# Delta-rule attention and an expert layer in one kernel: the first group's scores from stacked keys, half-block products in 64x64 tiles, other work order in the first steps

## The chip, the cores and the metric

The kernel runs on one core of one Trainium2 chip. The metric is the device time of one execution in microseconds. The time before is the median of three runs, 635.75 us (631.23 to 637.58). All data is 32-bit floating point; in the trace every matmul of the source stands as two matmul records and two weight loads.

## The reference, cut to what matters

Two parts follow one another. The first is a linear attention with the delta rule: for each of 4 batches and 8 heads a 48x48 state is walked over 768 tokens. Its output, 3072 rows of 384, is the input of the second part, in which each row goes to one of 8 experts (chosen by the largest gate logit) through two matrices with a ReLU between them.

```python
# attention: B, H, S, D = 4, 8, 768, 48
k_n = k / (norm(k) + 1e-06)
for t in range(S):
    y[t] = q[t] @ state
    v_old = state.T @ k_n[t]
    state = state + beta[t] * outer(k_n[t], v[t] - v_old)
# x = y as (3072, 384); experts: E = 8, F = 1024
expert = argmax(x @ w_gate); gate = softmax(x @ w_gate)[expert]
out = gate * (relu(x @ w1[expert]) @ w2[expert])
```

## The kernel before

The tokens are cut into 24 chunks of 32 (`C`), the chunks into groups of 4 (`GS`). A chunk is one **step**; the four batches lie on the 128 partitions, 32 tokens each. Per chunk and head a 32x32 triangular matrix, built from the products of the keys with each other, has to be inverted. VectorE does this for a group of 4 chunks at a time (`invert`), for all batches, tokens and heads side by side, in some seventy small operations, while the steps of the group ahead run. `fill` puts a number of microseconds of this work, by an estimate of its own, between the parts of a step.

The scores of a chunk are products of its keys with its keys (`k = 0`) and queries (`k = 1`), made by TensorE in 32x32 blocks. Two heads are stacked on 96 partitions; to keep them apart, the right-hand side is a "wide" copy with zeros where the other head's rows are. In the main loop those wide copies come from DRAM by DMA, half of each, into buffers that were zeroed once. For the first group, keys and queries are loaded as 48 partitions, one head each, and are not stacked:

```python
    def load_plain(c, k):
        t = kq_buffer()[0:D].rearrange("d p k t -> d (p k) t")
        for e, eng in enumerate((nc.sync, nc.scalar)):
            eng.dma_start(out=t[:, NP * e : NP * e + NP, :], in_=kq_t[c, D * e : D * e + D, :, k, :])
        return t
    ...
    def load_wide(c):
        if c < NS:
            for e in range(2):
                r = slice(D * e, D * e + D)
                nc.sync.dma_start(out=wide_kq[c % 3][r, e], in_=kq_t[c, r])
    ...
    def plain_scores(pa, keys, others):            # L348
        for h in range(H):
            for b in range(B):
                j = NP * (h % 2) + h // 2
                nc.tensor.matmul(
                    pa[rows_of(b), C * h : C * h + C], lhsT=keys[:, j, rows_of(b)],
                    rhs=others[:, j, rows_of(b)], start=True, stop=True, skip_group_check=True,
                )
    def front_scores(c, pa):                       # L359
        wide = wide_kq[c % 3]
        for p in range(NP):
            for b in range(B):
                for e in range(2):
                    nc.tensor.matmul(
                        pa[rows_of(b), 128 * p + 64 * e : 128 * p + 64 * e + 64],
                        lhsT=wide[:, e, p, 0, rows_of(b)], rhs=wide[:, e, p, :, rows_of(b)],
                        start=True, stop=True, skip_group_check=True,
                    )
        load_wide(c + 3)
        return c, pa
```

`scores` (L375) does the same for a later chunk with the stacked keys on the left. `keep_scores` (L399) and `keep_plain` (L388) mask the scores into `km` on VectorE.

The first group is inverted as two half blocks of 16. What lies between the halves is put together by `across`, with two small products per chunk on TensorE (L527), an eviction on ScalarE, and an addition on VectorE (L541). It runs as **chores**, one call at a time: for chunk 0 ahead of step 0, for chunks 1 to 3 within steps 0 to 2.

```python
        def product(l, r):
            po = psA.tile([128, 512], FP32, name="pa", tag="pa")
            for h in range(H):
                for b in range(B):
                    nc.tensor.matmul(
                        po[rows_of(b), W * h : W * h + W], lhsT=l[rows_of(b), H * s + h],
                        rhs=r[rows_of(b), h], start=True, stop=True, skip_group_check=True,
                    )
            return po[:, 0 : H * W]
```

`spread_out` (L558) then makes the block-diagonal copies `ubw` of the inverse on ScalarE, two operations for a whole group (for a chunk in the first group), each with a scale per partition of 0 or 1. A step begins with the values (`pv`, L595), takes off what the state holds (L609), evicts it as `R` (L620), multiplies by the inverse (`pz`, L631), evicts `Z` (L638), updates the state's sum (`acc`, L659) and the state (L667), and ends with the output (`pq`, L678), the scores of a later chunk and the start of the next step. The beginning of the kernel is this (shortened):

```python
    keys = [load_plain(c, 0) for c in range(GS)]
    ...                                            # constants, zeroing of the wide buffers
    for c in range(GS, GS + 3):
        load_wide(c)
    queries = [load_plain(c, 1) for c in range(GS)]
    ...
    for c in range(GS):
        ...
        plain_scores(pa, keys[c], keys[c])
        keep_plain(c, 0, pa[:, 0 : H * C], mask_0)
    behind.append([0, invert(0), 0.0])
    ahead = [front_scores(GS, acc[:, 2, :]), front_scores(GS + 1, acc[:, 3, :])]
    ...
    for c in range(GS):
        a = H * C * (c % 2)
        plain_scores(acc[:, c // 2, a : a + H * C], keys[c], queries[c])
    ...                                            # front_scores of GS + 2, GS + 3
    heat(3)                                        # L584: products of the identity, their result unused
    while not spread:
        fill(0.1)                                  # the inversion of group 0
    scale_v(0, 0); scale_v(0, 1)
    begin(0)
    chore()                                        # first half-block product
    ...
    chore(); ...; chore()                          # second product, addition
    spread_out((0, 1))
    ...
    for c in range(NS):
        ...
        extra = step(c)
        fill(4.0)
        ...
        more = score()
        if c + 1 < NS:
            begin(c + 1)
        fill(3.2)
        keep_scores(*more)
        if c == GS:                                # weights of expert 0, a piece per step
            weights[0] = start_w(wpool)
            pieces.extend(pieces_w(moe_w1[0], moe_w2[0], *weights[0]))
```

After the last step come the experts, one after another, on TensorE.

Of the kernel before, what the change touches and what calls it, by code (L numbers as in the profile page):

```python
# [31 lines left out]
E = 8  # L32
# [21 lines left out]
def _f32_consts():  # L54

    p = np.arange(128)[:, None]
    j = np.arange(128)[None, :]
    rev = np.broadcast_to(E - np.arange(E), (128, E))
    base = np.broadcast_to(np.arange(E) * LIST, (128, E))
    more = np.arange(E)[:, None] * LIST + CAP + np.arange(MAXR)[None, :] * 128
    more = np.broadcast_to(more.reshape(1, -1), (128, E * MAXR))
    t, w = p % C, j[:, :C]
    kk = 1.0 * (t == w) - (t < w)
    own = 1.0 * (p // C % 2 == np.arange(2)[None, :])
    half = t // (C // 2) == w // (C // 2)  # L70
    k0 = 1.0 * (t == w) - ((t < w) & half) - (t // (C // 2) > w // (C // 2))
    kq = -1.0 * (t < w)
    mine = -1.0 * (p // D == np.arange(2)[None, :])
    return np.concatenate(
        [kk, kq, k0, own, mine, rev, base, more, p < j, np.ones((128, 128))], axis=1
    ).astype(np.float32)
# [3 lines left out]
def kernel(  # L80
# [23 lines left out]
    CS = 3 * C + 4  # L104
# [3 lines left out]
    def part(w):  # L108
# [4 lines left out]
    mask, mask_0, own, mine, rev, base, further, upper, ones = (  # L113
        part(w) for w in (2 * C, C, 2, 2, E, E, E * MAXR, 128, 128)
# [164 lines left out]
    scored, front, now = [0], [None], [0]  # L279
# [34 lines left out]
    def load_plain(c, k):  # L314

        t = kq_buffer()[0:D].rearrange("d p k t -> d (p k) t")
        for e, eng in enumerate((nc.sync, nc.scalar)):
            eng.dma_start(out=t[:, NP * e : NP * e + NP, :], in_=kq_t[c, D * e : D * e + D, :, k, :])
        return t
# [6 lines left out]

    def load_wide(c):
        if c < NS:
            for e in range(2):
                r = slice(D * e, D * e + D)  # L330
                nc.sync.dma_start(out=wide_kq[c % 3][r, e], in_=kq_t[c, r])
# [11 lines left out]
    def plain_scores(pa, keys, others):  # L343

        for h in range(H):
            for b in range(B):
                j = NP * (h % 2) + h // 2
                nc.tensor.matmul(  # L348
                    pa[rows_of(b), C * h : C * h + C], lhsT=keys[:, j, rows_of(b)],
                    rhs=others[:, j, rows_of(b)], start=True, stop=True, skip_group_check=True,  # L350
                )

    def front_scores(c, pa):

        wide = wide_kq[c % 3]
        for p in range(NP):
            for b in range(B):
                for e in range(2):
                    nc.tensor.matmul(  # L359
                        pa[rows_of(b), 128 * p + 64 * e : 128 * p + 64 * e + 64],  # L360
                        lhsT=wide[:, e, p, 0, rows_of(b)], rhs=wide[:, e, p, :, rows_of(b)],
                        start=True, stop=True, skip_group_check=True,
                    )
        load_wide(c + 3)
        return c, pa

    def scores(c):

        if c >= NS:
            return None  # L370
        wide, kq = wide_kq[c % 3], kqs[c]
        pa = psA.tile([128, 512], FP32, name="pa", tag="pa")
        for p in range(NP):
            for b in range(B):
                nc.tensor.matmul(  # L375
                    pa[rows_of(b), 128 * p : 128 * p + 128], lhsT=kq[:, p, 0, rows_of(b)],
                    rhs=wide[:, :, p, :, rows_of(b)], start=True, stop=True,
                    skip_group_check=True,
                )
        load_wide(c + 3)  # L380
        return pa
# [135 lines left out]
    def across(gt, fdt, ub, s):  # L517

        W = C // 2
        part = ub[:, H * s : H * s + H, W:C]  # L520
        m1 = work.tile([128, H, W], FP32, name="m1")

        def product(l, r):
            po = psA.tile([128, 512], FP32, name="pa", tag="pa")
            for h in range(H):
                for b in range(B):
                    nc.tensor.matmul(  # L527
                        po[rows_of(b), W * h : W * h + W], lhsT=l[rows_of(b), H * s + h],
                        rhs=r[rows_of(b), h], start=True, stop=True, skip_group_check=True,
                    )  # L530
            return po[:, 0 : H * W]

        po = product(gt, part)
        nc.scalar.activation(out=m1[:].rearrange("p h w -> p (h w)"), in_=po, func=AF.Copy)

        def second():
            po = product(fdt, m1)
            chores.appendleft(partial(added, po))

        def added(po):  # L540
            nc.vector.tensor_tensor(  # L541
                out=part, in0=part, in1=po.rearrange("p (h w) -> p h w", h=H), op=OP.add
            )

        chores.appendleft(second)
# [5 lines left out]
    def spread_out(steps=(0, GS)):  # L551

        g, ub = spread[0]
        if g not in ubs:
            ubs[g] = block.tile([128, GS * H, 2, C], FP32, name="ubw")
        a, b = (H * s for s in steps)
        for k in range(2):
            nc.scalar.activation(  # L558
                out=ubs[g][:, a:b, k], in_=ub[:, a:b], func=AF.Copy, scale=own[:, k : k + 1]
            )  # L560
        if steps[1] == GS:
            spread.popleft()
# [38 lines left out]
    def step(c):  # L601
        g, s = divmod(c, GS)
        kq, ub, kt, vs, km = kqs.pop(c, None), ubs[g], kts.pop(c), vss.pop(c), kms[g]
# [38 lines left out]
        if c > 0:  # L642
            by_state(pq, 1, True)
        if c >= LATE:
            ranked()
            while turned:
                logits()
        if c == NS - 1:
            ahead_of_time(1)
        load_kq(c + LEAD + 1)  # L650
        if c < GS:
            load_kq(c + GS)
        extra = score() if c in EXTRA else None
        scale_v(c + 1, 1)
        if c < NS - 1:
# [10 lines left out]
            for e in range(2):  # L666
                nc.scalar.activation(  # L667
                    out=states[:, :, :, e], func=AF.Copy, scale=mine[0:DD, e : e + 1],
                    in_=acc[0:DD, :, 0:DM].rearrange(
                        "q b (p e w) -> q b p e w", p=NP, e=2  # L670
                    )[:, :, :, e],
                )
# [11 lines left out]
        if c == ss[0]:  # L684
            n = len(ss)
            xgs[c] = work.tile([128, n, ROW], FP32, name=f"xg{n}", bufs=3 if n == 1 else 2)
            lgs[c] = small.tile([128, GS, E], FP32, name="lg")
# [3 lines left out]
        if spread and GS <= c and c >= GS * (spread[0][0] - 1):  # L691
            spread_out()
        return extra

    def score():
        c = scored[0]
        scored[0] += 1
        return c, scores(c)
# [133 lines left out]
    keys = [load_plain(c, 0) for c in range(GS)]  # L832
    nc.scalar.dma_start(out=cf[:, 0:CS], in_=src[:, 0:CS])
    nc.scalar.dma_start(out=beta[:], in_=beta_blk)
    for i in (1, 2, 0):
        t = wide_kq[i][:].rearrange("q e p k w -> q (e p k w)")
        for j, eng in enumerate(((nc.vector, nc.gpsimd), (nc.gpsimd, nc.vector))[i % 2]):
            eng.memset(t[:, 1024 * j : 1024 * j + 1024], 0.0)
    for c in range(GS, GS + 3):
        load_wide(c)  # L840
    queries = [load_plain(c, 1) for c in range(GS)]
# [3 lines left out]
    load_vt(0)  # L845
    load_kt(0)
    for c in range(1, LEAD + 1):
        kqs[c] = kq_buffer()
    load_kq(1)

    kms[0] = km_buffer()
    for c in range(GS):
        pool, name = ((psA, "pa"), (psQ, "pq"), (psC, "pv"), (psC, "pz"))[c]
        pa = pool.tile([128, 512], FP32, name=name, tag=name)
        plain_scores(pa, keys[c], keys[c])
        keep_plain(c, 0, pa[:, 0 : H * C], mask_0)
    behind.append([0, invert(0), 0.0])
    ahead = [front_scores(GS, acc[:, 2, :]), front_scores(GS + 1, acc[:, 3, :])]
    load_vt(1)
    load_kt(1)  # L860
    for c in range(GS):
        a = H * C * (c % 2)
        plain_scores(acc[:, c // 2, a : a + H * C], keys[c], queries[c])
    load_kq(2)
    ahead.append(front_scores(GS + 2, psC.tile([128, 512], FP32, name="pv", tag="pv")))
    load_kq(8)
    ahead.append(front_scores(GS + 3, psQ.tile([128, 512], FP32, name="pq", tag="pq")))
    load_kq(9)
    load_kq(3)
    heat(3)  # L870
# [5 lines left out]
    chore()  # L876
    keep_plain(0, 1, acc[:, 0, :], mask[:, C : 2 * C])
# [4 lines left out]
    spread_out((0, 1))  # L882
# [12 lines left out]
    for c in range(NS):  # L895
# [3 lines left out]
        if c % GS == 0 and c // GS not in ubs:  # L899
            while not spread:  # L900
                fill(0.1)
            spread_out()
        extra = step(c)
        fill(4.0)
        if extra:
            keep_scores(*extra)
        if c < GS - 1:
            chore()
            spread_out((c + 1, c + 2))
# [9 lines left out]
        fill(3.2)  # L919
        keep_scores(*more)  # L920
        if c == GS:
# [193 lines left out]
```

## Time and profile before

| what | value |
|---|---|
| median of three runs | 635.75 us |
| span of the profiled execution | 630.8 us |
| step 0's first product (`pz`) starts | 43.71 us |
| `pz` of step 4 starts | 100.00 us |
| `Z` of the last step | 296.16 us |
| PE busy from 330 to 610 us | 279.73 of 280 us |
| VectorE busy from 0 to 297 us | 200.97 us |
| ScalarE busy from 0 to 44 us | 4.40 us |

The span has three parts. Up to 43.71 us is a prologue: loads, the scores of two groups, the inversion of the first. Then come 24 steps to about 297 us. Then, after an overlap of some 20 us, the experts, in which TensorE has no gap. A row of the profile names the line of the kernel, the engine, the operation, the tiles out and in, and the shape; "idle before" with a releaser says how long the engine stood before it and what ended the wait. The releaser "issue" means that nothing shown in the profile was waited for.

### The profile page before, as it was taken

Reading aid. Unit: us, or ns where it says so; the run is one execution under the profiler, and the core shown is the slowest. Engines: PE = TensorE matmul, PEld = TensorE weight load, DVE = VectorE, ACT = ScalarE, POOL = GpSimd, SP = SyncE. Lnnn points to the kernel's source line nnn. Section 1 sums busy time; section 2 is a strip of 40 time slices with the busy share of each in tenths; the row PEclk is TensorE's granted clock in tenths of the full one; section 3 lists DMA queues with packets and bytes.
Section 4 is the critical chain, followed back from the end, with each engine's and each line's share of the span. In section 5 each row is a group of like instructions: output and inputs, shape, how many; then the busy total and the mean of one; then the engine's idle time right before and its main releaser. Section 6 shows DMA issues by size and latency. Waiting matters only on the chain. (4 is left out here: it accounts for less than half of the span.)

```text
span 630.8 us, 17552 instructions
## 1 busy us (share of the span) xinstructions
PE 560.4 (89%) x7660; PEld 371.1 (59%) x7661; DVE 249.0 (39%) x818; ACT 184.2 (29%) x474; POOL 105.1 (17%) x111
## 2 busy tenths in 40 slices
PE   4378888879889899788999999999999999999990
PEld 4356666767767677566867555555555555455550
DVE  4845567997999979311410201111011110201100
ACT  0214536565465665563201101011011110111100
POOL 3000000010110202121137004014140231401011
PEclk9997758897888987685799999999999999999996
DMA  9857535676584322221017634223343223400000
GB/s 167 171 129 211 130 106 133 187 157 176 155 156 116 92 80 64 40 66 40 14 28 278 223 111 146 86 74 131 124 151 103 83 94 125 150 8 32 1 23 14
DMA packets 41632, 68.97 MB, mean 109 GB/s; under 512 B 10758, under 2 KB 31670, under 8 KB 41552
## 3 DMA queue, kind: packets, MB, share of 16 engines
q1 hardware_dynamic: 34128, 57.05, 33.4%
q0 software_dynamic: 4640, 9.47, 4.7%
q10 hardware_dynamic: 2784, 1.29, 1.2%
q8 instruction: 61, 1.00, 0.7%
q14 instruction: 19, 0.16, 0.1%
HBM read 59.02 MB, written 10.35 MB: 110 GB/s over the span
## 5 line engine op out<-in xcount | busy, mean ns | idle before, releaser
L993 PE MATMUL phe<-xTe,w1t 128*128 128x448 f32 (+1 forms) x384 | 136.2, 515 | 0.0
L1009 PE MATMUL pye<-w2t,hT 128*128 128x384 f32 x352 | 114.8, 486 | 0.0
L993 PEld LDWEIGHTS phe<-xTe,w1t 128*128 128x128 f32 x384 | 71.0, 190 | 60.4 <-issue 58.5
L1009 PEld LDWEIGHTS pye<-w2t,hT 128*128 128x128 f32 x352 | 66.9, 190 | 47.1 <-issue 2.6
L809 POOL DMA_INDIRECT lists<-ids,ri x24 | 24.0, 1001 | 277.8 <-DVE tmp L492 142.5
L998 DVE TENSOR_SCALAR hT<-phe 128x448 f32<-128x448 f32 (+1 forms) x32 | 18.9, 592 | 116.4 <-PE phe L993 104.3
L497 DVE TENSOR_TENSOR ut<-ut,tmp 128x58 f32<-128x58 f32 (+9 forms) x164 | 53.1, 324 | 5.4
L492 DVE TENSOR_TENSOR tmp<-ut 128x58 f32<-128x58 f32 (+9 forms) x164 | 52.8, 322 | 5.2
L180 POOL DMA_INDIRECT out_dram<-y,rows x22 | 21.9, 997 | 183.4 <-ACT y L1018 154.1
L571 ACT ACTIVATE vs<-vt,normt 128x48 f32<-128x48 f32 x192 | 47.9, 325 | 1.8 <-issue 1.8
L1002 ACT ACTIVATE hT<-phe 128x448 f32<-128x448 f32 (+1 forms) x32 | 16.6, 517 | 105.7 <-PE phe L993 105.7
L667 ACT ACTIVATE states<-acc,cf 96x768 f32<-96x768 f32 x46 | 38.7, 891 | 21.8 <-PE acc L659 19.4
L1018 ACT ACTIVATE y<-pye,xin 128x384 f32<-128x384 f32 x15 | 8.7, 581 | 122.5 <-PE pye L1009 122.5
L631 PE MATMUL pz<-R,ubw 64*64 64x48 f32 x736 | 29.9, 237 | 14.5 <-ACT lg L733 8.0
L988 DVE COPY xTe<-px 128x448 f32<-128x448 f32 (+1 forms) x24 | 13.3, 580 | 66.5 <-PE px L984 55.9
L631 PEld LDWEIGHTS pz<-R,ubw 64*64 64x64 f32 x736 | 26.8, 151 | 18.0 <-ACT lg L733 9.2
L678 PE MATMUL pq<-Z,km 32*32 32x48 f32 x1536 | 31.7, 230 | 6.3 <-issue 6.1
L678 PEld LDWEIGHTS pq<-Z,km 32*32 32x32 f32 x1536 | 25.5, 125 | 13.0 <-issue 12.6
L659 PE MATMUL acc<-Z,kt 32*96 32x96 f32 x736 | 29.1, 311 | 2.8 <-issue 1.5
L1014 DVE TENSOR_SCALAR y<-pye,xin 128x384 f32<-128x384 f32 x7 | 4.3, 618 | 68.3 <-PE pye L1009 68.3
L609 PEld LDWEIGHTS pv<-states,kq 96*32 96x32 f32 x736 | 17.4, 121 | 18.8 <-issue 11.7
L659 PEld LDWEIGHTS acc<-Z,kt 32*96 32x96 f32 x736 | 24.4, 210 | 6.4 <-issue 3.6
(142 smaller groups left out, 641.3 us busy)
## 6 DMA issues: line engine op xcount, KB each, us to landing
w1t<-in_moe_w_dram SPq DMA_DIRECT2D x7, 1536.0 KB, 12.3
w2t<-in_moe_w_dram SPq DMA_DIRECT2D x7, 1536.0 KB
kq<-in_kq_t_dram SPq DMA_DIRECT2D x23, 384.0 KB, 6.2
wkq<-in_kq_t_dram SPq DMA_DIRECT2D x40, 192.0 KB, 4.0
vt<-in_v_tok_dram SPq DMA_DIRECT2D x24, 192.0 KB, 2.9
kt<-in_k_tok_dram SPq DMA_DIRECT2D x24, 192.0 KB, 4.3
xs<-xg SPq DMA_DIRECT2D x24, 192.0 KB, 7.1
w1t<-in_moe_w_dram SPq DMA_DIRECT2D x6, 256.0 KB
```

What stands on the lines that cost most here:

```text
L180: nc.gpsimd.indirect_dma_start(out=out, out_offset=bass.IndirectOffsetOnAxis(ap=index, axis=0), in_=y[0:w, :], in_offset=None, bounds_chec ...
L492: nc.vector.tensor_tensor(out=tv, in0=ud[:, :, j + 1 : W, j].unsqueeze(3).to_broadcast([128, K, n, j]), in1=ud[:, :, j, 0:j].unsqueeze(2). ...
L497: nc.vector.tensor_tensor(out=ud[:, :, j + 1 : W, 0:j], in0=ud[:, :, j + 1 : W, 0:j], in1=tv, op=OP.add)
L571: nc.scalar.activation(out=vss[c][:, h, :], in_=vts[c][:, h, :], func=AF.Copy, scale=norms[g][:, H * s + h : H * s + h + 1],)
L631: nc.tensor.matmul(pz[r, D * h : D * h + D], lhsT=ub[r, H * s + h].rearrange("q k w -> q (k w)"), rhs=R[r, h, :], start=(h == 0), stop=Tru ...
L659: nc.tensor.matmul(acc[0:DD, b, DD * p : DD * p + DD], lhsT=kt[rows_of(b), 2 * p : 2 * p + 2, :], rhs=Z[rows_of(b), 2 * p : 2 * p + 2, :], ...
L667: nc.scalar.activation(out=states[:, :, :, e], func=AF.Copy, scale=mine[0:DD, e : e + 1], in_=acc[0:DD, :, 0:DM].rearrange("q b (p e w) -> ...
L678: nc.tensor.matmul(pq[rows_of(b), D * h : D * h + D], lhsT=km[rows_of(b), H * s + h, 1], rhs=Z[rows_of(b), h, :], start=(c == 0 and h == 0 ...
L809: nc.gpsimd.indirect_dma_start(out=lists, out_offset=bass.IndirectOffsetOnAxis(ap=ri[:, i : i + 1], axis=0), in_=ids[:, ss[i] : ss[i] + 1] ...
L993: nc.tensor.matmul(ph[:], lhsT=w1t[:, s, f * 128 : f * 128 + 128], rhs=xT[:, s, :], start=(s == 0), stop=(s == NK - 1),)
L998: nc.vector.tensor_scalar(out=hT[:, f, :], in0=ph[:], scalar1=0.0, scalar2=None, op0=OP.max)
L1009: nc.tensor.matmul(py[:], lhsT=hT[:, f, t * 128 : t * 128 + w], rhs=w2t[:, f, :], start=(f == 0), stop=(f == NF - 1),)
```

## The change

It does these things, all in the attention part:

- Keys and queries of the first group are loaded stacked on 96 partitions (`load_half`), into the buffers that the steps use later, so the second loading of chunks 1 to 3 goes. The wide copies for chunks 0 to 7 are made from them on chip: two operations with a scale of 0 or 1 per partition, on ScalarE, a few on VectorE. Zeroing the wide buffers and loading them from DRAM for chunks 4 to 7 go.
- All scores of the prologue then use the stacked form, with half as many matmuls.
- The half-block products take block-diagonal copies of the left side, made by `both` on ScalarE for chunk 0 and on GpSimd for chunks 1 to 3, and work in 64x64 tiles, with half as many matmuls.
- ScalarE's function table is loaded at the start by an operation on a dummy tile.
- Idle products (`heat`), to keep TensorE at work, are put in at waits: a fourth one in the prologue, three around the first half-block products and step 0, and one in each step that has no scores left to make.
- Up to step 9 `fill` takes 4.6 and 4.0 us of inversion per step in place of 4.0 and 3.2. The block-diagonal copies of the inverse are made chunk by chunk in every group. The first expert's weights are loaded from step 9 on instead of step 4.

```diff
+    def load_half(c, k, eng):
+        if c not in kqs:
+            kqs[c] = kq_buffer()
+        eng.dma_start(out=kqs[c][:, :, k, :], in_=kq_t[c, :, :, k, :])
...
+    def widen(c):
+        for e in range(2):
+            nc.scalar.activation(
+                out=wide_of(c)[:, e], in_=kqs[c][:], func=AF.Copy, scale=this[0:DD, e : e + 1]
+            )
...
+    def widen_half(c, k, w, i):
+        for e in range(2):
+            out, in_ = w[:, e, :, i, :], kqs[c][:, :, k, :]
+            if e or k:
+                nc.scalar.activation(out=out, in_=in_, func=AF.Copy, scale=this[0:DD, e : e + 1])
+            else:
+                nc.vector.tensor_scalar(
+                    out=out, in0=in_, scalar1=this[0:DD, 0:1], scalar2=None, op0=OP.mult
+                )
...
+    def half_scores(c, pa, w, i):
         for p in range(NP):
             for b in range(B):
+                nc.tensor.matmul(
+                    pa[rows_of(b), 64 * p : 64 * p + 64], lhsT=kqs[c][:, p, 0, rows_of(b)],
+                    rhs=w[:, :, p, i, rows_of(b)], start=True, stop=True, skip_group_check=True,
+                )
...
+        l1, l2 = (both(t[:, H * s : H * s + H], pool=s > 0) for t in (gt, fdt))
         def product(l, r):
             po = psA.tile([128, 512], FP32, name="pa", tag="pa")
             for h in range(H):
-                for b in range(B):
+                for q in two_of:
                     nc.tensor.matmul(
-                        po[rows_of(b), W * h : W * h + W], lhsT=l[rows_of(b), H * s + h],
-                        rhs=r[rows_of(b), h], start=True, stop=True, skip_group_check=True,
+                        po[q, W * h : W * h + W], lhsT=l[q, h].rearrange("q k w -> q (k w)"),
+                        rhs=r[q, h], start=True, stop=True, skip_group_check=True,
                     )
...
+    def both(of, out=None, pool=False):
+        if out is None:
+            out = work.tile([128, H, 2, C], FP32, name="bw", tag="bw", bufs=3)[:]
+        for k in range(2):
+            if pool:
+                nc.gpsimd.tensor_scalar(
+                    out=out[:, :, k], in0=of, scalar1=own[:, k : k + 1], scalar2=None, op0=OP.mult
+                )
+            else:
+                nc.scalar.activation(
+                    out=out[:, :, k], in_=of, func=AF.Copy, scale=own[:, k : k + 1]
+                )
+        return out
...
         if c > 0:
             by_state(pq, 1, True)
+        else:
+            heat(1, pq[:])
...
-        if spread and GS <= c and c >= GS * (spread[0][0] - 1):
-            spread_out()
+        if c >= GS - 1:
+            spread_out(c + 1)
...
     def score():
         c = scored[0]
         scored[0] += 1
+        if c >= NS:
+            heat()
         return c, scores(c)
...
     kms[0] = km_buffer()
+    w = (wide_kq[0], wide_kq[1])
     for c in range(GS):
+        if c % 2 == 0:
+            for i in range(2):
+                widen_half(c + i, 0, w[c // 2], i)
         ...
-        plain_scores(pa, keys[c], keys[c])
+        half_scores(c, pa, w[c // 2], c % 2)
         keep_plain(c, 0, pa[:, 0 : H * C], mask_0)
     behind.append([0, invert(0), 0.0])
...
-    heat(3)
+    heat(4)
     while not spread:
         fill(0.1)
     ...
     begin(0)
     chore()
+    heat(1, front[0][1][:])
     ...
     chore()
+    heat(1, front[0][1][:])
-    spread_out((0, 1))
+    spread_out(0)
...
-        fill(4.0)
+        fill(4.0 if c > LEAD else 4.6)
...
-        fill(3.2)
+        fill(3.2 if c > LEAD else 4.0)
...
-        if c == GS:
+        if c == LEAD:
```

## The prediction

> **What bounds the kernel now.** I read the page first, then the timeline of the first 60 us, then the table of windows cut at the steps, then the waits of VectorE.
>
> ```profile
> span 630.8 us, 17552 instructions
> PE 560.4 (89%) x7660; PEld 371.1 (59%) x7661; DVE 249.0 (39%) x818; ACT 184.2 (29%) x474; POOL 105.1 (17%) x111
> ...
> PEclk9997758897888987685799999999999999999996
> DMA  9857535676584322221017634223343223400000
> ...
> q8 instruction: 61, 1.00, 0.7%
> ```
>
> One slice is 15.8 us. TensorE ("PE") is near full from slice 19 on: that is the expert part, from about 320 us to 620 us, with the clock at 9 or more. The change touches no instruction there. So whatever it is worth lies before 300 us, in the attention part, and there PE's share is a poor guide: the clock digit drops to 5 and the DMA digit is 5 to 9 for the first twelve slices. The q8 line says that instructions themselves come by DMA: 1.00 MB in 61 packets is 16.4 KB a packet, and 7660 + 7661 PE instructions over 61 packets is 251 a packet, some 126 pairs of weight load and matmul.
>
> ```profile
> 11.80 0.68 PE L348 MATMUL pz<-kq 48*32 48x32 f32 x33 [2.11 <-issue]
> ...
> 12.41 3.13 PE L359 MATMUL acc<-wkq 96*32 96x64 f32 x93
> ...
> 18.30 1.38 PE L359 MATMUL acc<-wkq 96*32 96x64 f32 x35 [2.76 <-issue]
> ...
> 24.77 1.93 PE L348 MATMUL acc<-kq 48*32 48x32 f32 x128 [3.66 <-issue]
> ...
> 30.00 1.02 DVE L509 STREAM_TRANSPOSE fdt<-ut 128x512 f32<-128x512 f32 x1
> 30.97 0.74 PE L348 MATMUL acc<-kq 48*32 48x32 f32 x35 [4.26 <-issue]
> ...
> 36.08 4.39 PE L584 MATMUL pa<-ident 128*128 128x512 f32 x6
> ...
> 40.53 0.73 PE L527 MATMUL pa<-ub,km 32*32 32x16 f32 x64
> ...
> 42.42 0.29 DVE L541 TENSOR_TENSOR ub<-ub,pa 128x128 f32<-128x128 f32 x1 [8.79 <-PE pa L527]
> ...
> 43.71 1.14 PE L631 MATMUL pz<-vs,ubw 64*64 64x48 f32 x32 [1.34 <-ACT ubw L558]
> ```
>
> This is the prologue. VectorE ends the inversion of the first group at 31.02 us (30.00 + 1.02). The product that needs it (L527) starts at 40.53: 9.5 us later, although nothing it reads is missing. PE is in order and still works off scores and three heating products. Those are late because PE stops for 2.1 to 4.3 us with the releaser "issue", in the middle of runs of like matmuls, after exactly 128 pairs (93 + 35, then 128): a packet of instructions each. From 11.80 to 30.97 a packet takes 6.1 to 6.5 us while its 128 pairs need 2 to 4.5 us of work. So in the prologue **the instruction fetch of PE, behind a DMA that is 83 to 95% busy, sets the path**, and the 768 pairs of scores ahead of the heating (8 blocks of 64, 4 of them for queries, and 4 of 64 for the second group) are what is fetched.
>
> ```profile
> 44.00:57.37 13.37, 10.52 (x321) 8.03 (x317) 10.04 (x37) 5.96 (x17) 0.00 (x0) 0.62 0.80 217
> 57.37:71.81 14.44, 11.92 (x363) 9.17 (x364) 8.55 (x25) 6.46 (x19) 0.00 (x0) 0.76 0.45 118
> 71.81:87.80 15.99, 12.19 (x363) 9.29 (x363) 9.45 (x27) 6.45 (x19) 0.00 (x0) 0.76 0.49 136
> 87.80:100.00 12.20, 10.12 (x235) 8.21 (x235) 7.50 (x21) 7.35 (x18) 0.00 (x0) 0.75 0.42 116
> 100.00:109.30 9.30, 9.04 (x235) 7.34 (x235) 6.56 (x28) 5.39 (x16) 0.00 (x0) 0.82 0.48 126
> ```
>
> Columns: window, length, then PE, PEld, DVE, ACT, POOL busy with counts, clock, DMA share, GB/s. Steps 0 to 3 take 13.4, 14.4, 16.0 and 12.2 us; a later one takes 9 to 11. The long ones carry 128 extra pairs for the half-block products. The VectorE waits tell the rest:
>
> ```profile
> DVE ub L541 <- PE pa L527: 19.7, 4, 8.8
> ```
>
> 8.8 us of these 19.7 are the prologue's; the other 10.9 stand in steps 0 to 2 (1.5, 5.0, 4.4), where VectorE, in order, waits for the half-block product that PE does at a step's end, instead of inverting group 1. As a result group 1's inversion ends in step 3, and PE waits 2.1 us before step 4 for its copies.
>
> **What the Trainium skill says.** "Runtime: NRT & Kernel Launch", section "Instruction fetch mechanics": instructions are refilled in blocks of 16 KiB, 256 instructions, by a DMA of the sequencer's own, and the cost is mostly hidden. The trace agrees with the block (251 per packet) and not with "hidden" (the four gaps above are 12.8 us). "TensorE: Matmul & The Clock Gate", the part on the HAM clock gate: without sustained work the clock falls to half. Here the same pv<-vs product takes 0.91 us warm and 1.65 us cold, and the clock column is 0.62 to 0.76 in steps 0 to 3. "ScalarE: Activation LUTs", section "What ACT_TABLE_LOAD costs": about 1.28 us for a load; the trace has 1.28 us at 20.64, off the path, so moving it forward is worth nothing by itself.
>
> **The change part by part.**
>
> 1. Scores of group 0 and 1. Keys of two heads stacked on 96 rows instead of 48 halve the pairs: 4 x 64 becomes 4 x 32 for keys, the same for queries, and the second group's 4 x 64 becomes 4 x 32 of 128 columns. 768 pairs become 384, that is three packets less, 3 x 6.2 us of fetching. The DMA shrinks too: wide loads of 393 KB for chunks 4 to 7 go (1.57 MB) and so do the whole loads of chunks 1 to 3 (1.18 MB). At the 160 to 210 GB/s of the first windows 2.75 MB is about 14 us of DMA time, spread over 0 to 60 us.
>
> 2. ScalarE pays for it. A 128x1024 copy is 1.13 us (ubw, the row L558), a 128x256 one 0.49, so 0.83 ns an element and about 0.71 us for 512. Eight copies of 1024 are 9.0 us, four key copies of 512 are 2.8 us, eight for queries 5.7 us. ScalarE did nothing before 20.6 us, so this lies in idle time, but in a chain: keys land near 9 us, their last copy near 10, the copies of chunks 4 to 7 end near 19, of the queries near 25, the last scores near 26.
>
> 3. The start of the inversion. Before, it began at 12.98, because the last key block stood at 11.80 behind the first fetch. With 32 pairs a block, all key scores fit ahead of the point (223 pairs) where that fetch was needed. But each key has a copy of 0.7 us before it. I take 11.5 us, with the unchanged 18.0 us of VectorE: end near 29.5.
>
> 4. Heating and the first half-block product. Four products, by the measured 4.39 us for three, are 5.9 us: 26 to 32 us. So heating, not the inversion, is likely the last thing ahead of the product, by 2 us. Then product 0.6, its eviction 0.3, a heating product 1.2 to 1.5, second product 0.6, addition 0.3, copies 0.9: pz of step 0 near 35.3 instead of 43.7. **Gain 8.5 us**.
>
> 5. Steps 0 to 2. The half-block products in 64x64 tiles take 64 pairs a step instead of 128: half a packet, and a packet costs about 5.2 us here (14.44 us for 363 pairs, or 2.8 packets). That is 2.6 us a step, 7.8 in all, less about 1 us for the idle product put into step 0. The DMA carries 0.39 MB a step less. The mask copies go to POOL, which is empty here. VectorE now gets 4.6 + 4.0 us of inversion a step instead of 4.0 + 3.2; by the order of its instructions its half-block addition comes three pairs of operations later in step 1 and three in step 2, so of the 10.9 us of waiting I expect 3 to 4 to stay. Its own work, some 9.5 us a step, then bounds a step at about 11.5 us: (13.4 + 14.4 + 16.0) - 3 x 11.5 = **9.3 us**.
>
> 6. Step 3 and the copies for step 4. The last four transposes of group 1 stand before the masking of step 3 instead of around it, and the 2.19 us of copies are cut into 0.9 us per step. The 2.1 us before step 4 goes, giving 12.2 -> 10.7: **1.5 us**.
>
> 7. Steps 4 to 14. VectorE is 85 to 91% busy in 120 to 240 us, so these stay near 10 us. The first expert's weights move from steps 4 to 17 to steps 9 to 22, which frees DMA early and loads it late where its share was only 0.25 to 0.33: **0 to 2 us**.
>
> 8. Steps 15 to 23. A 512-column product is put in where the scores have run out, near 1.2 us warm. While VectorE bounds (to about 250 us) it is free; in the last four steps PE bounds and pays about 1 us each. Against that stand the 0.69 clock of 256 to 297 us: at half speed when cold, that is some 60% of the stretch cold. I set the sum at **0**, between +5 and -6.
>
> Sum: 8.5 + 9.3 + 1.5 + 1 + 0 = 20.3 us. 635.75 - 20.3 = 615.5; I say 616.
>
> **Rivals.** (a) ScalarE or the stacked keys' landing becomes the prologue's bound. For: the copies are a serial 17.5 us, and the 512-byte rows of the keys share the engines with rows of 4 KB. Against: 12 us of slack between 31.0 and 43.7. It would leave 4 of the 8.5 us, the total near 621. (b) Steps 0 to 3 are bound by VectorE alone and its waits only move to other products; then the halved pairs bring nothing and the total is near 624. For: VectorE still waits in order. Against: its busy time there is 7.5 to 10 us of 12 to 16. (c) The idle products cost their full 9 x 1.2 us late and never lift the clock: total near 625. (d) The clock does rise, and the cold half of 256 to 297 us shrinks: near 608.
>
> **Range and chances.** The prologue may miss by 3, steps 0 to 3 by 5, the late steps by 6, and the time before itself spans 631.23 to 637.58. Together about 9 us: 605 to 628. Faster by over 2% means under 623.0, which holds unless two rivals act together: 0.77. Within 2%: 0.21. Slower: 0.02.
>
> **What would show it.** pz<-vs,ubw of step 0 starts at 34 to 37 us; "issue" gaps on PE before it fall from four long ones to one or two; the addition of half blocks waits under 6 us in total; windows of steps 0 to 3 take 10.5 to 12.5 us; the step-4 wait for copies is gone; the clock in 256 to 297 us is at or above 0.75; and from the first expert on all is the same, only earlier. I am wrong if the heating ends after 34 us, if the keys land after 11 us, or if steps 4 to 15 grow because VectorE merely reaches its bound sooner and is then held up by ScalarE's copies each step.

## The result, and the profile after

The changed kernel takes 612.12 us (median of four runs, 609.67 to 614.43) where the kernel before takes 636.66 us (a fourth execution has joined the three of the start): a ratio of 0.963, 95% interval 0.955 to 0.970. The prediction was 616 us. In the two profiled executions the gain is 18.1 us of span, 630.8 to 612.7. The first lines are those of the page of the changed kernel that answer to the ones shown of before.

```profile
span 612.7 us, 16382 instructions
PE 560.7 (92%) x7046; PEld 364.4 (59%) x7047; DVE 248.2 (41%) x820; ACT 207.3 (34%) x529; POOL 113.7 (19%) x120
...
PEclk9998898987897888786999999999999999999996
DMA  8438465866663324431059124342243422500000
...
q8 instruction: 56, 0.92, 0.7%
```

PE is busy for as long as before (560.7 and 560.4 us) with 614 matmuls less; 56 instruction packets in place of 61. The DMA digits of the first three slices fell from 9, 8, 5 to 8, 4, 3. The clock digits of the fourth to the sixth slice were 7, 7, 5 and are 8, 8, 9. Next the timeline of the changed kernel's prologue.

```profile
12.42 0.72 ACT L348 ACTIVATE wkq<-kq,cf 96x512 f32<-96x512 f32 x1 [4.99 <-DMA kq<-in_kq_t_dram]
...
14.80 2.21 DVE L429 STREAM_TRANSPOSE ut<-km 128x256 f32<-128x256 f32 x4
...
23.22 4.27 PE L368 MATMUL acc<-wkq,kq 96*32 96x64 f32 x128
...
27.42 5.24 PE L608 MATMUL pa<-ident 128*128 128x512 f32 x8
...
31.91 1.07 DVE L517 STREAM_TRANSPOSE fdt<-ut 128x512 f32<-128x512 f32 x1
...
32.77 1.11 PE L536 MATMUL pa<-ub,bw 64*64 64x16 f32 x32
...
36.02 0.29 DVE L550 TENSOR_TENSOR ub<-ub,pa 128x128 f32<-128x128 f32 x1 [1.29 <-PE pa L536]
...
37.30 1.14 PE L655 MATMUL pz<-vs,ubw 64*64 64x48 f32 x32 [0.27 <-ACT ubw L570]
```

No score is split by an "issue" gap in this trace. Heating ends at 32.66 us (27.42 + 5.24) and the inversion at 32.98: the two meet, and the first product starts at 32.77, where before it started 9.5 us after the inversion's end. But the inversion starts at 14.80, later than before (12.98), because the last key's copy waited for its load until 12.42. Then the steps, in the table of windows of the changed kernel, with the columns as before.

```profile
37.30:52.28 14.98, 10.50 (x260) 7.72 (x260) 11.67 (x42) 6.06 (x17) 4.36 (x5) 0.77 0.80 191
52.28:63.22 10.94, 9.85 (x299) 8.13 (x299) 7.54 (x21) 6.45 (x19) 2.02 (x2) 1.00 0.66 171
63.22:76.11 12.89, 11.45 (x300) 8.92 (x300) 11.20 (x33) 6.45 (x19) 0.00 (x0) 0.87 0.38 112
76.11:83.95 7.84, 7.58 (x235) 6.07 (x235) 4.55 (x10) 6.17 (x18) 0.00 (x0) 1.00 0.56 152
```

Steps 1 to 3 are 3 to 4 us shorter each. Step 0 is longer than before, with a DMA share of 0.80, and the waits of PE name a new one, for the wide keys of a later chunk:

```profile
PE pa L382 <- DMA wkq<-in_kq_t_dram: 3.9, 1, 3.9
```

Cut at pz of steps 0, 4, 15 and 23, in the two profiled executions (the rows sum to the 18.1 us):

| stretch | before | after | difference |
|---|---|---|---|
| prologue | 43.71 | 37.30 | -6.4 |
| steps 0 to 3 | 56.29 | 46.65 | -9.6 |
| steps 4 to 14 | 111.10 | 109.33 | -1.8 |
| steps 15 to 22 | 83.07 | 83.81 | +0.7 |
| last step and experts | 336.6 | 335.6 | -1.0 |

### The profile page after: what moved, and what is told of

Same layout as the page of the kernel before. It is cut to its first block, busy times and chain, and to the rows that moved or that the text cites. A ratio compares the mean times of both kernels' runs of the same rounds, so it can differ in the third digit from the quotient of the medians.

```text
span 612.7 us, 16382 instructions
## 1 busy us (share of the span) xinstructions
PE 560.7 (92%) x7046; PEld 364.4 (59%) x7047; DVE 248.2 (41%) x820; ACT 207.3 (34%) x529; POOL 113.7 (19%) x120
## 3 DMA queue, kind: packets, MB, share of 16 engines
HBM read 56.66 MB, written 10.35 MB: 109 GB/s over the span
## 5 line engine op out<-in xcount | busy, mean ns | idle before, releaser
L655 PE MATMUL pz<-R,ubw 64*64 64x48 f32 x736 | 27.7, 227 | 10.4 <-ACT R L644 5.1
L655 PEld LDWEIGHTS pz<-R,ubw 64*64 64x64 f32 x736 | 24.7, 141 | 13.8 <-ACT R L644 7.4
L702 PE MATMUL pq<-Z,km 32*32 32x48 f32 x1536 | 27.9, 224 | 4.1 <-issue 4.1
L702 PEld LDWEIGHTS pq<-Z,km 32*32 32x32 f32 x1536 | 23.1, 121 | 7.4 <-issue 6.6
L683 PE MATMUL acc<-Z,kt 32*96 32x96 f32 x736 | 26.8, 292 | 0.0
L758 PE MATMUL pz<-wg,xT 128*128 128x8 f32 x144 | 21.3, 268 | 4.1 <-ACT pr L810 2.9
```

The lines of the kernel that those rows point to most:

```text
L655: nc.tensor.matmul(pz[r, D * h : D * h + D], lhsT=ub[r, H * s + h].rearrange("q k w -> q (k w)"), rhs=R[r, h, :], start=(h == 0), stop=Tru ...
L683: nc.tensor.matmul(acc[0:DD, b, DD * p : DD * p + DD], lhsT=kt[rows_of(b), 2 * p : 2 * p + 2, :], rhs=Z[rows_of(b), 2 * p : 2 * p + 2, :], ...
L702: nc.tensor.matmul(pq[rows_of(b), D * h : D * h + D], lhsT=km[rows_of(b), H * s + h, 1], rhs=Z[rows_of(b), h, :], start=(c == 0 and h == 0 ...
L758: nc.tensor.matmul(pt[:, LG : LG + E], lhsT=xT[:, s, :], rhs=wg[:, s, :], start=(s == 0), stop=(s == NK - 1), skip_group_check=True,)
```

## The experiments

The runs came in three sets, each on a chip of its own. The kernel before has a median of 634.8, 623.5 and 635.6 us there, and the changed kernel was measured again in the first and third set. So totals are compared inside a set, or by their ratio to the kernel before. The ratios leave disturbed executions out and the medians don't, so in the third set the two don't divide. The intervals of these ratios are about 0.010 to each side, so that no total is clear of the changed kernel's in the two sets that hold it. The stretch of steps 4 to 14 alone takes from 103.85 to 116.10 us in the traces of the changed kernel and its variants. The verdicts therefore rest on single stretches and waits of one trace per run.

**The changed kernel again**, in the first and in the third set.

> The changed kernel once more, on the chip of the next three. Theory and rivals alike: 609 to 615 us, 3.7% below the kernel before; pz of step 0 at 37 us, pz of step 4 at 84 us.

> The changed kernel again, as the reference of the next three on their chip: 0.963 to 0.970 of the kernel before.

612.73 us, ratio 0.970 (0.961 to 0.978), and 602.27 us, ratio 0.965 (0.955 to 0.975). Prologue 37.21 and 35.93, steps 0 to 3 43.24 and 43.45, step 0 alone 14.41 and 15.52 us. The short steps 1 to 3 and the long step 0 repeat.

**The double load taken out.**

```diff
-    for c in range(2 * GS, LEAD + 1):
-        load_kq(c)
-        load_vt(c - 2 * GS + 1)
-        load_kt(c - 2 * GS + 1)
+    load_kq(2 * GS)
+    load_vt(1)
+    load_kt(1)
+    for c in range(2 * GS + 1, LEAD + 1):
+        load_kq(c)
```

> The changed kernel with the loads of values and keys of chunk 2 left out of the prologue; step 0 loads them anyway, a second time, so nothing is missing. Theory: those two loads wait for buffers that step 0 frees (the second goes out at 41.3 us), and the wide keys of chunks 8 to 10 stand behind them in the same queue, so step 0's scores wait 3.9 us for their data. Then the wide loads go out near 28 us, the wait is gone, step 0 takes 11 us instead of 15.0 and the total falls by 3 to 4 us, to about 608. Rival: the DMA is simply full there (share 0.80 in step 0), the wait stays at 2 to 4 us, the total stays within 1 us.

608.23 us beside 612.73, ratio 0.957 (0.947 to 0.967). In the changed kernel the queue's timeline reads:

```profile
28.19 0.33 SPq L362 DMA_DIRECT2D vt<-in_v_tok_dram  x1
41.32 0.33 SPq L357 DMA_DIRECT2D kt<-in_k_tok_dram  x1
41.70 2.75 SPq L341 DMA_DIRECT2D wkq<-in_kq_t_dram  x6
```

and with the two loads out, the queue and the window of step 0:

```profile
26.16 3.77 SPq L341 DMA_DIRECT2D wkq<-in_kq_t_dram  x6
...
37.56:46.63 9.07, 8.46 (x260) 6.53 (x260) 8.32 (x31) 6.06 (x17) 4.36 (x5) 1.00 0.48 116
```

The keys of chunk 2 go out only when step 0 has read the buffer they need, and six wide loads stand behind them. The waits of the queue of the changed kernel say so; L683 is the product of step 0 that reads the keys:

```profile
SPq L357 <- PE acc L683: 12.7, 1, 12.7
```

With the two loads out the six go 15.5 us earlier, PE's wait for wide keys is gone, and step 0 takes 9.07 us instead of 14.41. That is 5.3 us, more than the wait alone, which is 3.7 us in the trace of the same set: PE is also busy for 1.65 us less, at a clock of 1.00 instead of 0.88. The rival, a DMA that is simply full, falls. The pages could have told of the double load: the reads from HBM fell from 59.02 to 56.66 MB, 0.39 MB less than the 2.75 MB that the prediction took off, and 0.39 MB are two loads of 192 KB. With them out it is 56.27 MB.

**Half-block products back in 32x32 tiles.**

```diff
-        l1, l2 = (both(...) for t in (gt, fdt))
...
-                for q in two_of:
+                for b in range(B):
...
```

> The changed kernel with the half-block products again in 32x32 tiles: 64 pairs each instead of 32, without the block-diagonal copies on ScalarE and GpSimd. A product took 0.73 to 1.06 us before and takes 1.07 to 1.17 us now, so the work itself is no longer than now; only the count of instructions doubles. Theory (instruction fetch bounds steps 0 to 2): 64 more pairs a step are half a packet, steps 0 to 2 grow by about 2 us each, the total by 4 to 7 us. Rival (VectorE and the clock bound them, the count is nothing): steps 0 to 2 the same within 0.7 us each, the total within 1.5 us or even lower.

618.99 us beside 612.73, ratio 0.975 (0.965 to 0.986). Steps 0, 1 and 2 take 13.78, 16.52 and 12.14 us, 42.4 in sum against 35.4 (same set) and 38.8 (first trace) of the changed kernel. The prologue is 1.7 us shorter: the copies leave ScalarE's chain, and a product takes 0.73 us in place of 1.11. In step 1:

```profile
51.92 0.42 PE L682 MATMUL acc<-Z,kt 32*96 32x96 f32 x8
54.45 0.76 PE L682 MATMUL acc<-Z,kt 32*96 32x96 f32 x24 [2.10 <-issue]
```

Gaps named issue add to 3.6 us over steps 0 to 2, again in the middle of like matmuls, where the changed kernel has 0.8 us in the same set and 2.0 us in the first trace. So the larger tiles don't make the product faster, they make it slower; what they save is instructions.

But the gaps are the smaller part of the 7.0 us by which the three steps differ inside the set. The half-block products take 5.0 us in them instead of 6.7, and PE is idle for 7.7 us instead of 5.7. The other 664 matmuls, the same in both, take 29.9 us instead of 23.1: the clock of steps 1 and 2 is 0.68 and 0.73 against 1.00. That the lower clock follows from the gaps is not shown. It came with the larger tiles too, and without any such gap: step 1 takes 15.67 us at 0.57 in the run with the keys in one queue, below.

**The old number of instructions in the prologue.** 384 pairs with one column each are added behind the four full scores.

```diff
         ahead.append((c, scores(c, pa)))
+        po = psA.tile([128, 512], FP32, name="pa", tag="pa")
+        for i in range(3):
+            for p in range(NP):
+                for b in range(B):
+                    nc.tensor.matmul(po[rows_of(b), p : p + 1], lhsT=kqs[c][:, p, 0, rows_of(b)],
+                                     rhs=kqs[c][:, p, 1, C * b : C * b + 1], ...)
```

> The changed kernel with 384 pairs of weight load and one-column matmul put in the prologue, 96 after each of the four full scores, into a PSUM tile that nothing reads. This gives the prologue back the number of PE instructions it had (768 pairs) without the data, the loads and nearly without the work: by the 0.73 us that 64 small pairs took, 96 pairs need about 1.1 us, and PE idles 0.6 to 1.0 us after each of these scores and longer before. Theory (fetch sets the prologue's PE): three more packets of 3.7 to 6.2 us each, with gaps named issue in the middle of runs; pz of step 0 moves from 37 to 42 us or later, the total grows by 4 to 8 us. Rival (PE was late because its keys and queries were late): at most 1 to 2 us more.

622.89 us beside 612.73, ratio 0.980 (0.970 to 0.991); pz of step 0 moved from 37.21 to 45.47 us. The timeline of PE:

```profile
19.83 1.02 PE L906 MATMUL pa<-kq 96*32 96x1 f32 x60
23.25 0.65 PE L906 MATMUL pa<-kq 96*32 96x1 f32 x34 [2.40 <-issue]
...
27.22 0.65 PE L906 MATMUL pa<-kq 96*32 96x1 f32 x35 [0.81 <-issue]
...
31.19 0.65 PE L906 MATMUL pa<-kq 96*32 96x1 f32 x35 [0.81 <-issue]
...
34.64 1.28 PE L368 MATMUL acc<-wkq,kq 96*32 96x64 f32 x37 [0.24 <-issue]
```

The gaps are back, and their ends are 3.97, 3.97 and 3.45 us apart with 128 pairs between: a packet each. They are shorter than before's 6.2 to 6.5 us; the DMA share between them is 0.03, 0.03 and 0.21. The heating ends 8.3 us later. 4.3 us are the four gaps; the other 4.0 are work that found no idle time, for 96 such pairs took some 1.5 us where I had reckoned 1.1. Fetch is shown to be a cost of its own; my number for this run put all of it there.

**Three idle products fewer, or nine.** One run leaves out the three at the half-block products and in step 0, one leaves out those of the late steps.

```diff
-        else:
-            heat(1, pq[:])
...
-    heat(1, front[0][1][:])          # twice
```

> The changed kernel without the three idle products between the first half-block products and in step 0 (the four ahead of them stay). Theory: each is longer (1.12 us) than the wait it fills, so the prologue ends 0.5 to 1.5 us earlier; steps 0 to 3 then run at the clock they get, and stay within 2 us in sum because instruction fetch and the late wide keys bound them. Rival: the clock of 0.77 to 1.00 in steps 0 to 3, against 0.63 to 0.76 before, is what made them shorter; without these products it falls back and steps 0 to 3 grow by 4 us or more.

598.34 us, ratio 0.967 (0.956 to 0.978): no gain and no loss. On the same chip, with the three in place (the run that follows), the prologue took 35.58 us and without them 34.72; step 0 took 15.35 us at a clock of 0.78 with, and 15.91 at 0.57 without. Steps 0 to 3 took 47.88 us in sum with and 45.54 without, so the growth of 4 us that the rival named is absent. The wide keys come late in both, so this says little of what the products are worth when the keys are in time.

```diff
         scored[0] += 1
-        if c >= NS:
-            heat()
```

> The changed kernel without the idle product that each step from 15 on gets where no scores are left. Prediction's step 8: they cost about 1 us each in the steps that PE bounds and give it back by a higher clock, so the total is the same within 4 us; the clock of the last four steps falls from 0.88 to about 0.7. Rival c: they only cost, and without them the total falls by 6 to 9 us. Rival d: they carry the late steps, without them the total grows by 5 us or more.

597.12 us, ratio 0.960 (0.949 to 0.971). Steps 15 to 22 take 69.97 us at a clock of 0.90, against 73.15, 74.22 and 76.27 us at 0.91, 0.93 and 0.87 in the three other runs of the set. So the products don't carry these steps. They may cost some of what rival c named: the stretch is 3 to 6 us shorter without them in single traces, and the interval of the total is too wide to tell.

**The keys in one queue.**

```diff
-        load_half(c, 0, (nc.sync, nc.scalar)[c % 2])
+        load_half(c, 0, nc.sync)
```

> The changed kernel with all four key loads in the sync engine's queue, ahead of everything else in it, where the changed kernel puts every second one in ScalarE's queue. Theory: the fourth key landed at 12.4 us because its rows of 512 bytes took turns, in the other queue, with rows of 4 KB of the chunks 4 to 7 that are not needed yet. In one queue all four keys land by 8 to 9.5 us, the inversion starts 2.5 to 3.5 us earlier (11.5 instead of 14.8), but the four heating products, which ended at 32.7 us beside an inversion that ended at 33.0, then are the last thing: pz of step 0 comes 1 to 2 us earlier and the total falls by 1 to 2 us. Rival (the DMA is simply full until 12 us): the key lands at 11.5 to 12.5 us as before, nothing changes.

595.51 us, ratio 0.953 (0.943 to 0.962), but inconclusive: on this chip the inversion began at 10.99 and 11.95 us with the old order and at 10.88 with the new one. The late key that was to be mended (an inversion that began at 14.4 to 15.7 us, in the first trace and all four of the first set) does not occur here. What the rows of 4 KB do to it where it occurs stays open. The trace shows something else. The first product of step 0 starts at 33.45 us, earlier than in the set's other traces with the old loads of chunk 2 (35.58 and 34.72), and then step 0 is the longest of all traces, and step 1 the longest with 64x64 tiles:

```profile
33.45:51.83 18.38, 15.35 (x262) 11.63 (x261) 11.82 (x42) 6.07 (x17) 3.77 (x5) 0.50 0.63 161
51.83:67.50 15.67, 15.40 (x299) 12.90 (x300) 7.92 (x22) 6.45 (x19) 1.83 (x2) 0.57 0.41 112
```

All idle products are in place here, and still the clock falls to 0.5 at 31.1 us and stays there until 65.3, the last 13 us of this with PE busy nearly throughout. Ahead of the fall PE stood idle for 1.63 us, because the heating had ended at 26.58 and its next product waited for the inversion until 28.20. A like wait of 1.44 us in the run with the double load taken out left the clock at 1.00. So what sets the clock is not known from these runs, and idle products alone don't secure it.

**Both mends.** 

> The changed kernel with both mends of the load order: no second load of chunk 2's values and keys in the prologue, and all four key loads in one queue. Theory: the gains add, 4 to 5 us from the first and 1 to 2 from the second: 605 to 608 us where the changed kernel takes 612, a ratio of 0.950 to 0.957 to the kernel before. Rival: VectorE bounds steps 4 to 15 and gives the second back: the same as the first alone, ratio 0.957.

591.38 us, ratio 0.951 (0.942 to 0.960). Prologue 35.56, step 0 9.09 us, beside 15.35 and 15.91 in the two runs of the set with the old loads: the first mend works on another chip too. In nine traces with the double load step 0 takes 13.77 to 18.38 us. The second mend shows no gain: with the old order of the keys, the prologue took 35.58 and 34.72 us on this chip.

**The old amounts of VectorE work per step.**

```diff
-        fill(4.0 if c > LEAD else 4.6)
-        fill(3.2 if c > LEAD else 4.0)
+        fill(4.0)
+        fill(3.2)
```

> The changed kernel with 4.0 and 3.2 us of inversion per step in all steps, in place of 4.6 and 4.0 up to step 9. Theory: this is what took the wait ahead of step 4: with the old amounts group 1's last transposes and copies come inside step 3 again, step 3 grows from 7.8 to 10 us or more, and the total grows by 2 to 4 us. Rival (PE's instructions bound steps 0 to 3, VectorE has room): step 3 grows by under 1 us, the total is the same within 1.5 us.

610.86 us beside 602.27, ratio 0.977 (0.967 to 0.988). Steps 0 to 3 take 48.32 us against 43.45, step 3 alone 10.36 against 7.81. The waits of ScalarE from 60 to 100 us show why:

```profile
ACT ubw L570 <- DVE ub L512: 3.6, 1, 3.6
```

The copies for step 4 wait again for the last transposes. The theory named 2 to 4 us of the total; 2.6 stand in step 3, 4.9 in the four steps, 8.6 in the medians. Of the rest, 3.0 us lie in step 1, at a clock of 0.72 instead of 1.00; that it has to do with the amounts is not shown.

**A shorter prologue on top of both mends.** Heating cut from four to two, none between the half-block products, chunk 0 in 32x32 tiles.

```diff
+        two = s > 0
+        parts = two_of if two else [rows_of(b) for b in range(B)]
...
-    heat(4)
+    heat(2)
```

> The changed kernel with both mends of the load order, two heating products in place of four, none between the first half-block products and in step 0, and chunk 0's half-block products in 32x32 tiles straight from the masked scores, without ScalarE's copies; chunks 1 to 3 stay in 64x64 tiles with GpSimd's copies. Theory: the heating no longer ends after the inversion, a first product takes 0.73 instead of 1.11 us, the copies of about 0.9 us leave the chain: pz of step 0 comes 3 us earlier than in the version with the two mends alone, step 0 takes 9 us, and the total is 0.943 to 0.951 of the kernel before. Rival (VectorE bounds steps 4 to 15 and the clock is lower without heat): 0.950 to 0.957, no better than the two mends alone, which were at 0.951.

599.97 us beside the changed kernel's 602.27, ratio 0.956 (0.945 to 0.966). pz of step 0 starts at 31.64 us, 3.9 earlier than with both mends alone. And step 0, in the window of this kernel and then of the one with both mends:

```profile
31.64:44.62 12.98, 11.62 (x258) 9.95 (x258) 10.21 (x36) 6.07 (x17) 4.37 (x5) 0.61 0.34 90
```

```profile
35.56:44.65 9.09, 8.48 (x261) 6.55 (x261) 8.33 (x32) 6.08 (x17) 4.38 (x5) 1.00 0.49 127
```

With one idle product fewer the step takes 12.98 us at a clock of 0.61, in place of 9.09 us at 1.00, and PE is busy for 3.1 us longer in it. Step 1 starts at 44.62 and 44.65 us: the 3.9 us won in the prologue are lost in step 0, and the total is where the rival put it. The run changes five idle products and the tiles of chunk 0 at once, so it doesn't tell which of them the clock hangs on. (The two are from different chips; the inversions began at 10.49 and 10.30 us, so the difference doesn't come from the loads.) Without them in the late steps too:

> The version before this one without the idle product in the steps from 15 on. Prediction's step 8: the same within 4 us. By the steps 15 to 23 of the run without them (70 us where three runs with them had 73 to 76) it could be 3 us faster; by the clock, as much slower.

600.22 us, ratio 0.955 (0.943 to 0.967), the same again. The fastest version by its ratio is the one with the two mends and all idle products, 0.951; it wasn't run beside the changed kernel on one chip. The first mend alone was, and there it takes 608.23 us against 612.73, with ranges that overlap (601.40 to 612.48 and 610.46 to 619.18).

## Why the prediction was right, and where not

Predicted 616 us with a gain of 20.3 us; measured 612.12 us. In the profiled pair the gain is 18.1 us, and by the sum of the steps it comes from where it was placed: 19.3 us were given to the prologue and steps 0 to 3, and 16.0 us lie there.

- **Fetch as the prologue's bound**: right. The four gaps are gone with the instructions, and four come back with 384 added pairs. The packets themselves stand in the traces: in the kernel before, instruction packets of 16384 bytes have landed at 10.10, 16.58, 23.33 and 29.57 us, and PE goes on at 11.80, 18.30, 24.77 and 30.97, each time 1.4 to 1.7 us later; with the added pairs it is 1.3 to 1.6 us. On the third set's chip the changed kernel has one such gap left:

```profile
24.10 1.29 PE L368 MATMUL acc<-wkq,kq 96*32 96x64 f32 x37 [1.81 <-issue]
```

- **The DMA behind the fetch**: right in part. A packet took 6.2 to 6.5 us from gap to gap, not 6.1. The DMA was full during the first three of these gaps (a share of 0.88 or more in every microsecond from 10 to 28), but from 29 us on it moved nothing, and the fourth gap lasted until 30.97. The next packet, still in the kernel before, had an almost empty DMA (share 0.03):

```profile
30.97:34.71 3.74, 3.46 (x127) 3.16 (x128) 1.94 (x4) 0.00 (x0) 0.00 (x0) 1.00 0.03 7
```

So a packet takes 3.5 to 4.0 us here without other traffic, and about 2.5 us more (6.2 less 3.7) with it: after PE went on, the next packet went out 3.25 to 3.50 us later with a full DMA and 1.41 us later with an empty one. The count in the prediction needs a correction too: between the gaps at 11.80 and 18.30 lie 126 pairs (33 + 93). The 128 are the 35 from 18.30 on and another row of 93 that it doesn't show.
- **Step 3 of the working, the start of the inversion**: wrong in the first trace, 14.80 us where I had 11.5. The term "keys land near 9 us" failed: 12.4. I had taken it from the row where the fourth key's first half lands before, though the loads around it changed. "Keys after 11 us" stood among the prediction's signs of being wrong, and it came. On the two other chips the start was 10.8 to 12.8 us with the same order of loads.
- **Step 4, heating as the last thing**: the products ended at 32.66 us, as reckoned (32), and the inversion beside them at 32.98. 8.5 us became 6.4. Of the 2.0 us by which pz came after 35.3, 0.6 to 0.9 are a slip in the sum: the terms listed behind the heating add to 3.9 to 4.2 us, which puts pz at 35.9 to 36.2. 0.7 us are the later end of the heating. The rest is the chain from the first product to pz, 4.5 us measured, in which each of the two half-block products takes 1.11 us where 0.6 was put. pz at 37.30 is just outside the 34 to 37 that were given as a sign.
- **Step 5, steps 0 to 2**: 9.3 us predicted, 5.3 measured (13.66 + 14.44 + 15.99 less 14.98 + 10.94 + 12.89). Steps 1 and 2 gave 6.6. The failing term is step 0, put at 11.5 us: the wait for the wide keys of chunk 8, which the order of the loads brings in, I had not seen, though the order of the sync engine's loads could be read from the diff. VectorE as the bound of 11.5 us a step did not hold either: step 1 takes 10.94 us with VectorE busy for 7.54, and step 0 takes 9.07 once its keys are in time. The waits of VectorE for half blocks fell from 10.9 us in steps 0 to 2 to 3.6 (4.9 less the prologue's 1.29), as said, and the gaps named issue from 6.6 us to 2.0.
- **The clock, which the sum leaves out**: in steps 1 to 3 of the first pair of traces, the 235 matmuls that each step has besides the half-block products took 31.6 us before and 25.2 after. PE's idle time fell from 8.4 to 2.8 us, and the half-block products took 1.0 us longer. So of the 11.0 us that these steps gave, 6.4 came with the clock (0.75 to 0.76 before, 1.00, 0.87 and 1.00 after), no less than from shorter waits. What raised it is not shown; the run with the keys in one queue has the same program in step 1 and took 15.67 us for it.
- **Step 6, step 3 of the kernel**: 1.5 us predicted, 4.4 measured. The mechanism holds, as the run with the old amounts shows (2.6 us). The clock is in it as well: PE's busy time in this step fell from 10.12 to 7.58 us for the same 235 matmuls.
- **Steps 7 and 8**: 1 and 0 us predicted, 1.8 and -0.7 measured. That is inside what these stretches differ between runs. The clock from 256 to 297 us rose from 0.69 to 0.83, as the prediction's sign asked, and still steps 15 to 22 were not shorter. The late weights were not tried apart.
- **The rivals**: (b) is not wholly excluded: the 32x32 tiles bring gaps of 1.6 to 2.8 us more back, and the rest of their cost came with a lower clock. (d) falls with the run without late products; (c) in full does not fit the 612.12 us, but some cost of the late products stays possible. (a) names a delay that did occur, but it cost little: with the inversion starting at 10.82 us in the third set, pz still began at 35.93 us, as heating then came last; that is 1.4 us less than 37.30.

That the total came within 4 us of the number is therefore partly luck: the wait in step 0, which the prediction had not seen, took away 3.5 us (14.98 less 11.5), and the clock, which it had not counted, gave 6.4 us. The prologue is the part that was right, in the main, for the reason given.

## What to carry to other kernels

Count instructions as a load of their own: where runs of small matmuls stop in the middle at equal counts, fewer and larger ones can help even if each takes longer. After moving loads forward, read the queue in its order: one load that waits for a buffer holds up all that stand behind it, and a load done twice is easily overlooked. An idle product ahead of a stretch of small matmuls can be worth what it costs, and it can fail to hold the clock; so look at the granted clock of the stretch behind it before putting it in or taking it out.

## What was not expected of the hardware

A 64x64 half-block product of 32 pairs took 1.11 us, the 32x32 one of 64 pairs 0.73 when its instructions were there. PE went on 1.3 to 1.7 us after the landing of the instruction packet it had stood for in the prologues, also with an empty DMA. GpSimd needed 0.91 us for a masked copy of 128x256, ScalarE 0.49. With the same program the inversion began at 14.8 and 15.2 us in two traces and at 10.8 us on another chip, by the landing of one load.
